# Convolution lanes moved by one 512-token window, with the tap sums begun as their products come

## The chip, the core and the metric

The kernel runs on one core of one Trainium2 chip. The metric is the device time of one execution in microseconds (us), taken as the median of several runs; a profile of one execution, taken by the hardware profiler, lies beside it. The names used below: TensorE (PE in the profile; PEld is its weight load), VectorE (DVE), ScalarE (ACT), GpSimd (POOL) and SyncE (SP), which here only issues DMAs. SBUF is the on-chip memory, PSUM the memory that TensorE writes its results to.

## The reference

The input `x` has 8 sequences of 4096 tokens with 192 channels in float32. First comes a causal convolution over 7 tokens: the 8 heads have 24 channels each, and every head has 7 tap weights, which go through a softmax. Then comes a gated layer on every token:

```
w   = softmax(weight, axis=-1)                      # 8 heads x 7 taps
y_t = sum over k of w[head, k] * x[t - 6 + k]       # zeros ahead of a sequence
out = (relu(y @ w_gate) * (y @ w_val)) @ w_out      # 192 -> 1536 -> 192
```

The output has 32768 rows of 192 values in float32.

## The kernel before, in words

**Tiling.** A window is 512 tokens (`WIN`, line 40). A unit is two windows of one sequence together with the same two windows of the sequence four further on (`UNIT`, line 51), so that 64 channels of either sequence fill the 128 partitions. There are 16 units (`NUNIT`, line 52); four units go through one pair of sequences. The 192 channels are three chunks of 64 (`NCH`).

**A unit on TensorE** has two stages. In the *gate stage* `gate_val` (line 540) goes through two windows; in each, 12 groups of 24 matmuls (line 560) build the gate and the value product of 128 hidden features in two PSUM tiles; ACT takes the relu of one (line 571) and DVE multiplies it with the other into `hT` (line 572). In the *projection stage* `project_turn` (line 575) is called six times, for three output blocks `p` in two turns each, in the order of line 703; each call is 48 matmuls (line 582). After a block's first turn ACT copies two columns (`between_turns`, line 594); after its second, DVE transposes the block out of PSUM (`turn_out`, line 597, its instruction is line 600). `store` (line 605) writes the unit's output through SP. All PSUM tiles come from one pool of four in rotation (line 70).

**The convolution.** TensorE does it for the first two units: `conv_steps` (line 372) for the two windows of unit 0, and `conv` (line 401, its matmuls line 409, its ACT moves line 422, its transposing DMAs line 441) for unit 1, conv(2) for the first 560 tokens ahead of unit 0's projections and conv(3) for the rest between two of them (line 710). From unit 2 on a *lane* does it on the other engines. The lane of unit u+2 runs beside the projections of unit u:

- `lane_load` (line 241) loads x into `x_e` by POOL's DMA queue (line 250); `lane_turn` (line 446) takes 16 tokens of halo from the unit before (line 452), reorders on POOL (line 462) and transposes by eight DMAs on SP (line 464) into `x_r`: channels on partitions, tokens along the row.
- The 3 x 1024 values of a partition are split at `LDVE` = 1280. For the first 1280, ACT writes tap 0 into `acc` (`lane_first`, line 506, instruction line 510) and DVE adds taps 1 to 6 in place (`lane_rest`, line 517), two instructions a tap, of 1024 and 256 elements (line 521): out = x_r * tap + acc, both tensors in SBUF. The sixth tap writes the result into `xc`.
- For the other 1792, ACT writes the product of each tap into its own buffer (`product`, line 486, instruction line 490, two instructions of 768 and 1024 elements), and POOL sums the seven buffers by six additions of 1792 elements (`add`, line 497, instruction line 499), the last of them into `xc`. DVE does the 768-element piece of tap 0 as the last step of its lane (line 531).

**What sets the order.** Nothing reorders: each engine runs its instructions in program order (line 61) and waits by semaphores for data and for free buffers. `TAPS` (line 44) says which products ACT issues after each block's first turn, here taps 6 and 5, then 4 and 3, then 2, 1 and 0; `STEPS` (line 43) says how many of DVE's 13 lane steps stand ahead of each `turn_out`: 6, 5 and 2. POOL's sums for unit u+1 are issued in unit u's part of the main loop (lines 661 to 681), the last one behind the gate stage (line 685); tap 0 being the last product, with DVE's piece the last of its lane, the first sum waits for DVE's line 531. POOL's loads and reorderings stand between these sums in its queue. Each product has one buffer, one `acc` exists, `x_r` has two buffers and `xc` three. In the last two units there is no lane.

Of the kernel before, what the change touches and what calls it, by code (L numbers as in the profile page):

```python
# [15 lines left out]
def kernel(  # L16
# [27 lines left out]
    TAPS = [(6, 5), (4, 3), (2, 1, 0)]  # L44
# [13 lines left out]
    second = [min(t, 2 * UNIT - SUB) for t in range(UNIT, 2 * UNIT, SUB)]  # L58
    GROUPS += [(0, second[:GSUB]), (0, second[GSUB:])]

# [18 lines left out]
    def load_x(g, streams=range(2)):  # L79
# [25 lines left out]
        apool.tile([128, FLAT - LDVE], FP, name=f"prod{jj + 1}")[:, 0 : 2 * D] for jj in range(GSUB)  # L105
# [135 lines left out]
    def lane_load(u, streams=range(2)):  # L241


        bp, t0 = u * UNIT // S, u * UNIT % S
        if u not in xes:
            xes[u] = epool.tile([128, TILES, 2, NCH, 64], F16, name="x_e"), None
        xe, head = xes[u]
        for st in streams:
            row = (bp + NB * st) * S + t0
            nc.gpsimd.dma_start(  # L250
                out=xe[:, :, st, :, :].rearrange("p j c r -> p j (c r)"),
                in_=bass.AP(
                    tensor=x.tensor,
                    offset=x.offset + row * D,
                    ap=[[D, 128], [128 * D, TILES], [1, D]],
                ),
            )
        if 1 in streams and t0 and u - 1 not in xes and u - 1 not in xrs:
            head = const.tile([HALO, 2, NCH, 64], F16, name="head")
            nc.gpsimd.dma_start(  # L260
                out=head[:].rearrange("p s c r -> p s (c r)"),
                in_=bass.AP(
                    tensor=x.tensor,
                    offset=x.offset + (bp * S + t0 - HALO) * D,
                    ap=[[D, HALO], [NB * S * D, 2], [1, D]],
                ),
            )
        xes[u] = xe, head
# [10 lines left out]
    lane_load(2, range(1))  # L279
    for s in (8, 9):  # L280
        pool_halves(s)
    lane_load(2, range(1, 2))
# [82 lines left out]
    xc = {}  # L365
# [30 lines left out]
    def evict(copy, g, ps, c):  # L396
        copy(out=xc[0][:, c, WIN * g : WIN * (g + 1)], in_=ps[:, 0, :])

    def conv(g):
# [40 lines left out]
        for jj, t in enumerate(toks):  # L440
            nc.sync.dma_start_transpose(
                out=xc[1][:, :, t - UNIT : t - UNIT + SUB],
                in_=y[0:SUB, jj].rearrange("p c s r -> p (c s r)"),
            )

    def lane_turn(u):
        xe, head = xes.pop(u)
        xr = rpool.tile([128, NCH, HALO + UNIT], F16, name="x_r")
        if u * UNIT % S == 0:
            nc.gpsimd.memset(xr[:, :, 0:HALO], 0.0)  # L450
        elif head is None:
            nc.gpsimd.tensor_copy(out=xr[:, :, 0:HALO], in_=xrs[u - 1][:, :, UNIT : UNIT + HALO])
        else:
            turned = const.tile([HALO, NCH, 2, 64], F16, name="turned")
            for st in range(2):
                nc.gpsimd.tensor_copy(out=turned[:, :, st, :], in_=head[:, st, :, :])
            nc.sync.dma_start_transpose(
                out=xr[:, :, 0:HALO], in_=turned[:].rearrange("p c s r -> p (c s r)")
            )
        xp = epool.tile([128, TILES, NCH, 2, 64], F16, name="x_p")  # L460
        for st in range(2):
            nc.gpsimd.tensor_copy(out=xp[:, :, :, st, :], in_=xe[:, :, st, :, :])  # L462
        for j in range(TILES):
            nc.sync.dma_start_transpose(
                out=xr[:, :, HALO + 128 * j : HALO + 128 * j + 128],
                in_=xp[:, j].rearrange("p c s r -> p (c s r)"),
            )
        xrs[u] = xr

    def pieces(lo, hi):  # L470


        while lo < hi:
            c, t = lo // UNIT, lo % UNIT
            n = min(UNIT - t, hi - lo)
            yield lo, n, c, t
            lo += n

    def shifted(u, c, k, t, n):
        o = HALO - KW + 1 + k + t  # L480
        return xrs[u][:, c, o : o + n]

    def flat(u):
        return xc[u][:].rearrange("p c t -> p (c t)")

    def product(u, k):
        prods[u, k] = apool.tile([128, FLAT - LDVE], FP, name=f"prod{k}")
        for at, n, c, t in pieces(LDVE, FLAT):
            if k or t == 0:
                nc.scalar.activation(  # L490
                    out=prods[u, k][:, at - LDVE : at - LDVE + n],
                    in_=shifted(u, c, k, t, n),
                    func=ACTF.Copy,
                    scale=tap[:, c, k : k + 1],
                )

    def add(u, k):
        p0 = prods[u, 0]
        nc.gpsimd.tensor_tensor(  # L499
            out=p0[:] if k < KW - 1 else flat(u)[:, LDVE:FLAT],  # L500
            in0=p0[:],
            in1=prods.pop((u, k))[:],
            op=ALU.add,
        )

    def lane_first(u):
        accs[u] = apool.tile([128, LDVE], FP, name="acc")
        xc[u] = xcpool.tile([128, NCH, UNIT], F16, name="xc")
        for at, n, c, t in pieces(0, LDVE):
            nc.scalar.activation(  # L510
                out=accs[u][:, at : at + n],
                in_=shifted(u, c, 0, t, n),
                func=ACTF.Copy,
                scale=tap[:, c, 0:1],
            )

    def lane_rest(u):
        acc = accs.pop(u)
        for k in range(1, KW):
            for at, n, c, t in pieces(0, LDVE):  # L520
                nc.vector.scalar_tensor_tensor(  # L521
                    out=(flat(u) if k == KW - 1 else acc)[:, at : at + n],
                    in0=shifted(u, c, k, t, n),
                    scalar=tap[:, c, k : k + 1],
                    in1=acc[:, at : at + n],
                    op0=ALU.mult,
                    op1=ALU.add,
                )
                yield
        at, n, c, t = next(pieces(LDVE, FLAT))  # L530
        nc.vector.tensor_scalar(  # L531
            out=prods[u, 0][:, 0:n],
            in0=shifted(u, c, 0, t, n),
            scalar1=tap[:, c, 0:1],
            scalar2=None,
            op0=ALU.mult,
        )
        yield

    def gate_val(u, w):  # L540
        h = hpool.tile([128, NFF, 2, WIN], F16, name="hT")
        xcb = xc[u]
        for f in range(NFF):
# [12 lines left out]
            for i, c in order:  # L556
                W = (Wg, Wv)[i]
                for q in range(0, 128, M):
                    for st in range(2):
                        nc.tensor.matmul(  # L560
                            out=pss[i][q : q + M, st, :],
                            lhsT=W[64 * st : 64 * st + 64, c, 128 * f + q : 128 * f + q + M],
                            rhs=xcb[64 * st : 64 * st + 64, c, WIN * w : WIN * (w + 1)],
                            start=(c == 0),
                            stop=(c == NCH - 1),
                            tile_position=(64 * st, q),
                            skip_group_check=True,
                        )
# [76 lines left out]
    xc[0] = xcpool.tile([128, NCH, UNIT], F16, name="xc")  # L645
# [10 lines left out]
    loaded = apool.tile([128, FLAT - LDVE], FP, name="prod0")  # L656
# [4 lines left out]
    for u in range(NUNIT):  # L661
        lane = 1 <= u < NUNIT - 1
        if lane:
            add(u + 1, 1)
        if u == 1:
            lane_load(3)
            add(2, 2)
            add(2, 3)
        if u + 2 < NUNIT:
            lane_turn(u + 2)  # L670
        if u == 0:
            xts[3] = load_x(3)
# [15 lines left out]
        if u == 0:  # L688
            xc[1] = xcpool.tile([128, NCH, UNIT], F16, name="xc")
            conv(2)  # L690
        del xc[u]
# [11 lines left out]
        for p, turn in ((0, 0), (1, 0), (0, 1), (2, 0), (1, 1), (2, 1)):  # L703
# [16 lines left out]
            turn_out(tiles[p], o, p)  # L720
        store(o, bp, w0)
# [30 lines left out]
```

## Time and profile before

| what | value |
|---|---|
| time, median of 3 runs | 763.53 us (763.51 to 763.62) |
| span of the profiled execution | 761.2 us |
| the rest of the time, outside the span | 2.33 us |
| HBM read and written | 29.40 MB, 25.17 MB |
| gate products on DVE, 128x1024 | 383, mean 1221 ns |
| relus on ACT, 128x1024 | 383, mean 1023 ns |
| sums on POOL, 128x1792 | 84, mean 3993 to 4001 ns |
| moves of conv(2) and conv(3) on ACT | 10, 4.6 us together |

The span runs from the first to the last instruction of the profiled execution; the time also has what lies around it. Line numbers (L499) are those of the kernel above. In a timeline row stand the start, the duration, the engine, the line, the operation, and what it writes and reads; rows of neighbours of one kind are merged (x6), and a bracket gives the idle time ahead and what ended it. In a table of stages each engine has its busy time and, in brackets, its instructions; then come the granted clock of TensorE, the share of DMA time and GB/s. A matmul's end is modelled, so a busy TensorE is read by the length of its stages rather than by its busy share.

### The profile page before, as it was taken

Reading aid. Unit: us, or ns where it says so; the run is one execution under the profiler, and the core shown is the slowest. Engines: PE = TensorE matmul, PEld = TensorE weight load, DVE = VectorE, ACT = ScalarE, POOL = GpSimd, SP = SyncE. Lnnn points to the kernel's source line nnn. Section 1 sums busy time; section 2 is a strip of 40 time slices with the busy share of each in tenths; the row PEclk is TensorE's granted clock in tenths of the full one; section 3 lists DMA queues with packets and bytes.
Section 4 is the critical chain, followed back from the end, with each engine's and each line's share of the span. In section 5 each row is a group of like instructions: output and inputs, shape, how many; then the busy total and the mean of one; then the engine's idle time right before and its main releaser. Section 6 shows DMA issues by size and latency. Waiting matters only on the chain.

```text
span 761.2 us, 30408 instructions
## 1 busy us (share of the span) xinstructions
PE 757.1 (99%) x13732; PEld 497.5 (65%) x13732; DVE 669.9 (88%) x634; ACT 604.0 (79%) x671; POOL 425.0 (56%) x200
## 2 busy tenths in 40 slices
PE   9999999999999999999999999999999999999998
PEld 5556666666666666666666666666666666666668
DVE  7879989998998989989899899998999989896691
ACT  7898887878878788787877878788797887874471
POOL 8608749094591936829277391864909558092000
PEclk9999999999999999999999999999999999999999
DMA  9927536054450534516255152442715432030302
GB/s 149 154 56 131 85 82 86 5 121 49 95 76 6 126 42 98 72 27 119 28 106 65 48 102 23 111 59 70 88 14 121 49 88 42 3 84 3 86 3 84
DMA packets 154513, 54.36 MB, mean 71 GB/s; under 512 B 149632, under 2 KB 154384, under 8 KB 154384
## 3 DMA queue, kind: packets, MB, share of 16 engines
q1 hardware_dynamic: 117600, 37.87, 22.6%
q0 software_dynamic: 36352, 14.26, 17.1%
q8 instruction: 107, 1.75, 0.9%
q10 hardware_dynamic: 432, 0.30, 0.1%
q14 instruction: 22, 0.18, 0.1%
HBM read 29.40 MB, written 25.17 MB: 72 GB/s over the span
## 4 chain that ended last, share of the span: by engine, by line
PE 99%; DMA 0%; ACT 0%; issue 0%
PE ps L560 65%; PE ps L582 31%; PE ps L625 2%; PE ps L386 0%; PE ps L409 0%; DMA w<-in_weight_dram 0%; PE ps L195 0%; PE ps L330 0%; PE ps L211 0%; PE ps L205 0%; ACT out_s L636 0%; ACT L129 0%
## 5 line engine op out<-in xcount | busy, mean ns | idle before, releaser
L572 DVE TENSOR_TENSOR hT<-gr,ps 128x1024 f16<-128x1024 f16 (+1 forms) x385 | 468.9, 1218 | 35.3 <-ACT gr L571 8.3
L571 ACT ACTIVATE gr<-ps 128x1024 f16<-128x1024 f32 (+1 forms) x385 | 392.8, 1021 | 116.5 <-PE ps L560 116.5
L499 POOL TENSOR_TENSOR prod<-prod,prod 128x1792 f32<-128x1792 f32 x70 | 279.5, 3993 | 258.6 <-DVE prod L531 230.8
L560 PE MATMUL ps<-xc,Wg 64*64 64x512 f16 (+1 forms) x4464 | 324.3, 376 | 0.0
L560 PE MATMUL ps<-xc,Wv 64*64 64x512 f16 (+1 forms) x4464 | 324.2, 376 | 0.0
L582 PE MATMUL ps<-hT,Wo 64*64 64x512 f16 x4320 | 236.3, 376 | 0.0
L560 PEld LDWEIGHTS <-Wg 64*64 64x64 f16 (+1 forms) x4464 | 163.5, 107 | 85.2
L560 PEld LDWEIGHTS <-Wv 64*64 64x64 f16 (+1 forms) x4464 | 157.0, 106 | 91.4 <-DVE hT L572 0.3
L582 PEld LDWEIGHTS <-Wo 64*64 64x64 f16 x4320 | 153.9, 107 | 78.9 <-issue 0.3
L490 ACT ACTIVATE prod<-x_r,tap 128x1024 f32<-128x1024 f16 (+1 forms) x182 | 175.1, 1044 | 0.0
L521 DVE SCALAR_TENSOR_TENSOR acc<-x_r,tap,acc 128x1024 f32<-128x1024 f16 (+1 forms) x140 | 113.2, 874 | 2.0 <-ACT acc L510 2.0
L600 DVE STREAM_TRANSPOSE out_s<-ps 128x1024 f32<-128x1024 f32 x45 | 56.1, 1247 | 33.3 <-PE ps L582 28.8
L499 POOL TENSOR_TENSOR xc<-prod,prod 128x1792 f16<-128x1792 f32 x14 | 56.0, 4001 | 0.4
L462 POOL COPY x_p<-x_e 128x1536 f16<-128x1536 f16 x28 | 40.3, 1463 | 0.1
L250 POOL DMA_DIRECT2D x_e<-in_x_dram x28 | 25.5, 911 | 0.0
L595 ACT COPY turned_by<-ps 128x2 f32<-128x2 f32 x45 | 7.0, 156 | 21.8 <-PE ps L582 19.9
L521 DVE SCALAR_TENSOR_TENSOR xc<-x_r,tap,acc 128x1024 f16<-128x1024 f16 (+1 forms) x28 | 24.1, 859 | 0.0
L510 ACT ACTIVATE acc<-x_r,tap 128x1024 f32<-128x1024 f16 (+1 forms) x28 | 21.6, 821 | 0.0
L625 PEld LDWEIGHTS <-hT 128*128 128x128 f16 x192 | 15.8, 98 | 0.4 <-issue 0.4
L625 PE MATMUL ps<-Wo,hT 128*128 128x192 f16 x192 | 16.0, 246 | 0.0
L636 ACT COPY out_s<-ps 128x768 f32<-128x768 f32 (+2 forms) x5 | 3.2, 638 | 12.7 <-PE ps L625 12.7
L636 DVE COPY out_s<-ps 128x192 f32<-128x192 f32 x1 | 0.4, 356 | 13.3 <-PE ps L625 13.3
(58 smaller groups left out, 72.4 us busy)
## 6 DMA issues: line engine op xcount, KB each, us to landing
out_dram<-out_s SPq DMA_DIRECT2D x121, 192.0 KB
x_e<-in_x_dram POOLq DMA_DIRECT2D x28, 384.0 KB, 5.3
x_r<-x_p SPq DMA_TRANSPOSE x112
out_dram<-out_s SPq DMA_DIRECT2D x3, 384.0 KB
out_s<-in_x_dram POOLq DMA_DIRECT2D x4, 240.0 KB, 6.7
prod<-in_moe_w_out_dram POOLq DMA_DIRECT2D x1, 576.0 KB, 9.1
prod<-in_x_dram SPq DMA_DIRECT2D x2, 192.0 KB
out_s<-in_x_dram POOLq DMA_DIRECT2D x2, 192.0 KB, 4.9
```

The lines of the kernel that those rows point to most:

```text
L250: nc.gpsimd.dma_start(out=xe[:, :, st, :, :].rearrange("p j c r -> p j (c r)"), in_=bass.AP(tensor=x.tensor, offset=x.offset + row * D, ap ...
L462: nc.gpsimd.tensor_copy(out=xp[:, :, :, st, :], in_=xe[:, :, st, :, :])
L490: nc.scalar.activation(out=prods[u, k][:, at - LDVE : at - LDVE + n], in_=shifted(u, c, k, t, n), func=ACTF.Copy, scale=tap[:, c, k : k + 1],)
L499: nc.gpsimd.tensor_tensor(out=p0[:] if k < KW - 1 else flat(u)[:, LDVE:FLAT], in0=p0[:], in1=prods.pop((u, k))[:], op=ALU.add,)
L510: nc.scalar.activation(out=accs[u][:, at : at + n], in_=shifted(u, c, 0, t, n), func=ACTF.Copy, scale=tap[:, c, 0:1],)
L521: nc.vector.scalar_tensor_tensor(out=(flat(u) if k == KW - 1 else acc)[:, at : at + n], in0=shifted(u, c, k, t, n), scalar=tap[:, c, k : k ...
L560: nc.tensor.matmul(out=pss[i][q : q + M, st, :], lhsT=W[64 * st : 64 * st + 64, c, 128 * f + q : 128 * f + q + M], rhs=xcb[64 * st : 64 * ...
L571: nc.scalar.activation(out=gr[:, sts], in_=pss[0][:, sts], func=ACTF.Relu)
L572: nc.vector.tensor_tensor(out=h[:, f, sts], in0=gr[:, sts], in1=pss[1][:, sts], op=ALU.mult)
L582: nc.tensor.matmul(out=ps[64 * st : 64 * st + 64, b, :], lhsT=Wo[64 * r : 64 * r + 64, f, p, :], rhs=hs[b][64 * r : 64 * r + 64, f, st, :] ...
L600: nc.vector.transpose(out=o[:].rearrange("p t (b d) -> p b t d", b=2)[:, :, :, 32 * p : 32 * p + 32], in_=ps[:].rearrange("p b (t c) -> p ...
L625: nc.tensor.matmul(out=ps[:, i // 2, D * (i % 2) : D * (i % 2) + D], lhsT=h[:, f, st, 128 * q : 128 * (q + 1)], rhs=Wo[:, f, :, :].rearran ...
```

## The change

The lane works on *blocks* of two windows that are shifted by one window against the units: block b has the windows 2b+3 and 2b+4, that is the second window of unit b+1 and the first of unit b+2. There are 15 blocks (0 to 14), and the last has one window, so that the lanes do 29 windows where they did 28. conv(3) goes: TensorE convolves window 2 with conv(2), and window 3 comes from block 0. The lane of block u runs beside the projections of unit u, as the lane of unit u+2 did; its first window is now needed by the second window of the next unit's gate stage, where before the next gate stage had to pass altogether.

The products are issued in tap order: 0 and 1 after the first block's first turn, 2 and 3, then 4 to 6. DVE's piece is that of tap 6. The sums stand in POOL's queue behind all else of the unit, at the end of its turn of the main loop; each waits for its product. The last sum is two instructions of 896 elements, one a window. The next block's reordering and the load of the one after it are issued behind the unit's gate stage, ahead of the sums. Tiles keep their sizes; the window becomes an outer dimension of the accesses (2 x 512, 2 x 128, 2 x 384), and a block that crosses from one sequence to the next has 16 zeros between its windows in `x_r`.

```
-    TAPS = [(6, 5), (4, 3), (2, 1, 0)]
+    TAPS = [(0, 1), (2, 3), (4, 5, 6)]
...
-    FLAT = NCH * UNIT
-    LDVE = 1280
+    LDVE = 640
+    LPOOL = NCH * WIN - LDVE
+    CUT = LDVE - WIN
...
+    NBLOCK = NUNIT - 1
...
+    def windows(b):
+        return [k for k in (2 * b + 3, 2 * b + 4) if k < 2 * NUNIT]
...
+    def second_start(b):
+        return HALO + WIN + HALO * (WIN * (2 * b + 4) % S == 0)
...
+    MINE = [(0, 0, 0, WIN), (WIN, 1, 0, CUT)]
+    POOLS = [(0, 1, CUT, WIN - CUT), (WIN - CUT, 2, 0, WIN)]
...
+    def add(b, k):
+        p0, pk = prods[b, 0], prods.pop((b, k))
+        if k < KW - 1:
+            end = LPOOL * len(windows(b))
+            nc.gpsimd.tensor_tensor(out=p0[:, 0:end], in0=p0[:, 0:end], in1=pk[:, 0:end], op=ALU.add)
+            return
+        for w in range(len(windows(b))):
+            part = slice(LPOOL * w, LPOOL * (w + 1))
+            nc.gpsimd.tensor_tensor(
+                out=xcs[b][:, w, :, :].rearrange("p c t -> p (c t)")[:, LDVE : NCH * WIN],
+                in0=p0[:, part],
+                in1=pk[:, part],
+                op=ALU.add,
+            )
...
+    def window(u, w):
+        if u == 0:
+            return dense[0], w
+        if w == 1:
+            return xcs[u - 1], 0
+        return (xcs[u - 2], 1) if u > 1 else (dense[1], 0)
...
     for u in range(NUNIT):
-        lane = 1 <= u < NUNIT - 1
-        if lane:
-            add(u + 1, 1)
-        if u == 1:
-            lane_load(3)
-            add(2, 2)
-            add(2, 3)
-        if u + 2 < NUNIT:
-            lane_turn(u + 2)
         if u == 0:
-            xts[3] = load_x(3)
+            lane_turn(0)
+            lane_load(1)
...
-        if lane:
-            for k in range(4 if u == 1 else 2, KW - 1):
-                if k == KW - 2 and 1 < u < NUNIT - 3:
-                    lane_load(u + 3, range(1))
-                add(u + 1, k)
-            if 1 < u < NUNIT - 3:
-                lane_load(u + 3, range(1, 2))
         hs = [gate_val(u, w) for w in range(2)]
-        if lane:
-            add(u + 1, KW - 1)
-        if u == 1:
-            lane_load(4)
...
-        if u + 2 < NUNIT:
-            lane_first(u + 2)
-            lane = lane_rest(u + 2)
+        if u < NBLOCK:
+            lane_first(u)
+            lane = lane_rest(u)
+        if u + 1 < NBLOCK:
+            lane_turn(u + 1)
+        if u + 2 < NBLOCK:
+            lane_load(u + 2)
...
                 between_turns(tiles[p])
-                if u == 0 and p == 0:
-                    conv(3)
                 if lane:
                     for k in TAPS[p]:
-                        product(u + 2, k)
-                if u == 0 and p == 1:
-                    psum.tile([128, 2, 512], FP, name="ps")
+                        product(u, k)
...
             turn_out(tiles[p], o, p)
+        if lane:
+            for k in range(1, KW):
+                add(u, k)
         store(o, bp, w0)
```

In the kernel after the change the lines that the prediction names stand elsewhere: sums L517 and, for the last, L521; multiply-adds L543; DVE's product piece L554; products L506; gate products L603; transposes out of PSUM L631.

More of the change, by code (lines that the diff above doesn't have):

```diff
@@ L104 @@
     raw = [
-        apool.tile([128, FLAT - LDVE], FP, name=f"prod{jj + 1}")[:, 0 : 2 * D] for jj in range(GSUB)
+        apool.tile([128, 2 * LPOOL], FP, name=f"prod{jj + 1}")[:, 0 : 2 * D] for jj in range(GSUB)
     ]
@@ L239, with lane_load @@
     xes, xrs, accs, prods = {}, {}, {}, {}
[L241 to L247, printed above, removed]
+    def windows(b):
+        return [k for k in (2 * b + 3, 2 * b + 4) if k < 2 * NUNIT]
+    def lane_load(b, streams=range(2)):
+        n = 4 * len(windows(b))
+        if b not in xes:
+            xes[b] = epool.tile([128, TILES, 2, NCH, 64], F16, name="x_e"), None
+        xe, head = xes[b]
         for st in streams:
-            row = (bp + NB * st) * S + t0
+            row = NB * st * S + WIN * (2 * b + 3)
             nc.gpsimd.dma_start(
-                out=xe[:, :, st, :, :].rearrange("p j c r -> p j (c r)"),
+                out=xe[:, 0:n, st, :, :].rearrange("p j c r -> p j (c r)"),
                 in_=bass.AP(
@@ L278 @@
         pool_halves(s)
-    lane_load(2, range(1))
+    lane_load(0, range(1))
     for s in (8, 9):
         pool_halves(s)
-    lane_load(2, range(1, 2))
+    lane_load(0, range(1, 2))
     mx = const.tile([128, 1], FP)
@@ L396, in evict @@
     def evict(copy, g, ps, c):
-        copy(out=xc[0][:, c, WIN * g : WIN * (g + 1)], in_=ps[:, 0, :])
+        copy(out=dense[0][:, g, c, :], in_=ps[:, 0, :])
     def conv(g):
@@ L459, in lane_turn @@
             )
+        at = second_start(b)
+        if at > HALO + WIN:
+            nc.gpsimd.memset(xr[:, :, at - HALO : at], 0.0)
+        n = 4 * len(windows(b))
         xp = epool.tile([128, TILES, NCH, 2, 64], F16, name="x_p")
         for st in range(2):
-            nc.gpsimd.tensor_copy(out=xp[:, :, :, st, :], in_=xe[:, :, st, :, :])
-        for j in range(TILES):
+            nc.gpsimd.tensor_copy(out=xp[:, 0:n, :, st, :], in_=xe[:, 0:n, st, :, :])
+        for j in range(n):
+            to = HALO + 128 * j if j < 4 else at + 128 * (j - 4)
@@ L464, in lane_turn @@
             nc.sync.dma_start_transpose(
-                out=xr[:, :, HALO + 128 * j : HALO + 128 * j + 128],
+                out=xr[:, :, to : to + 128],
                 in_=xp[:, j].rearrange("p c s r -> p (c s r)"),
             )
[L468 to L503, printed above, removed]
-        )
[L506 to L512, printed above, removed]
+        xrs[b] = xr
@@ new lines, in shifted, with both, result @@
+    def shifted(b, c, k, t, n):
+        o = 1 - KW + k + t
+        row = xrs[b][:, c, HALO + o : HALO + o + n]
+        return bass.AP(
+            tensor=row.tensor,
+            offset=row.offset,
+            ap=[row.ap[0], [second_start(b) - HALO, len(windows(b))], [1, n]],
+        )
+    def both(tile, b, lo, n):
+        return tile[:].rearrange("p (w t) -> p w t", w=2)[:, 0 : len(windows(b)), lo : lo + n]
+    def result(b, lo, n):
+        return xcs[b][:].rearrange("p w c t -> p w (c t)")[:, 0 : len(windows(b)), lo : lo + n]
@@ new lines, with product @@
+    MINE = [(0, 0, 0, WIN), (WIN, 1, 0, CUT)]
+    POOLS = [(0, 1, CUT, WIN - CUT), (WIN - CUT, 2, 0, WIN)]
+    def product(b, k):
+        prods[b, k] = apool.tile([128, 2 * LPOOL], FP, name=f"prod{k}")
+        for at, c, t, n in POOLS[k == KW - 1 :]:
+            nc.scalar.activation(
+                out=both(prods[b, k], b, at, n),
+                in_=shifted(b, c, k, t, n),
+                func=ACTF.Copy,
+                scale=tap[:, c, k : k + 1],
+            )
[12 more added lines that the diff above has]
+                op=ALU.add,
+            )
@@ L513, in lane_first @@
+    def lane_first(b):
+        accs[b] = apool.tile([128, 2 * LDVE], FP, name="acc")
+        xcs[b] = xcpool.tile([128, 2, NCH, WIN], F16, name="xc")
+        for at, c, t, n in MINE:
+            nc.scalar.activation(
+                out=both(accs[b], b, at, n),
+                in_=shifted(b, c, 0, t, n),
                 func=ACTF.Copy,
@@ L529, in lane_rest @@
                 yield
-        at, n, c, t = next(pieces(LDVE, FLAT))
+        k = KW - 1
+        at, c, t, n = POOLS[0]
         nc.vector.tensor_scalar(
-            out=prods[u, 0][:, 0:n],
-            in0=shifted(u, c, 0, t, n),
-            scalar1=tap[:, c, 0:1],
+            out=both(prods[b, k], b, at, n),
+            in0=shifted(b, c, k, t, n),
+            scalar1=tap[:, c, k : k + 1],
             scalar2=None,
```

51 lines of the change are left out of this document (24 added, 27 removed).

## The prediction

> **What bounds the kernel now.** I read the page's engine table first, then the clock row, then the chain that ended last.
>
> ```profile
> span 761.2 us, 30408 instructions
> PE 757.1 (99%) x13732; PEld 497.5 (65%) x13732; DVE 669.9 (88%) x634; ACT 604.0 (79%) x671; POOL 425.0 (56%) x200
> PEclk9999999999999999999999999999999999999999
> PE 99%; DMA 0%; ACT 0%; issue 0%
> ```
>
> TensorE is busy from end to end at the full granted clock, and the chain is TensorE alone. The chain in order of time shows how regular that is; the first four rows are unit 0's projection stage, then the gate stage of unit 1, one later unit and the start of the next, and the gate stage of unit 15.
>
> ```profile
> 40.56 0.99 PE ps L409 x8
> 41.55 2.71 PE ps L582 x48
> 44.27 0.96 PE ps L409 x8
> 45.22 13.07 PE ps L582 x240
> 58.30 31.13 PE ps L560 x576
> ...
> 384.70 31.08 PE ps L560 x576
> 415.78 15.54 PE ps L582 x288
> 431.32 31.08 PE ps L560 x576
> ...
> 711.04 31.08 PE ps L560 x576
> ```
>
> A unit is 31.08 us of gate and value matmuls (two windows of 15.54) and 15.54 us of projection, 46.62 together; the first and the last of the 15 gate stages after unit 0 differ by 0.05. So a gain can only come from matmuls that go, and a loss only from a wait that reaches TensorE. The other engines decide whether one does. Their busy time in the two stages of that unit, then line 499 (POOL's sums) alone, then line 521 (DVE's multiply-adds) alone:
>
> ```profile
> 384.70:415.78 31.08, 31.08 (x580) 20.34 (x576) 28.96 (x25) 24.13 (x24) 28.62 (x11) 1.00 0.61 104
> 415.78:431.32 15.54, 15.54 (x292) 10.42 (x288) 14.02 (x17) 14.47 (x19) 0.00 (x0) 1.00 0.01 3
> ...
> 384.70:415.78 31.08, 23.98 (x6) 1.00 0.61 104
> 415.78:431.32 15.54, 0.00 (x0) 1.00 0.01 3
> ...
> 384.70:415.78 31.08, 0.00 (x0) 1.00 0.61 104
> 415.78:431.32 15.54, 9.72 (x12) 1.00 0.01 3
> ```
>
> The columns are PE, PEld, DVE, ACT, POOL. DVE (14.02 of 15.54) and ACT (14.47) are nearly full in the projection stage, and POOL does nothing there. All six sums lie in the gate stage, all twelve multiply-adds in the projection stage: they never meet.
>
> **What goes: a half convolution on TensorE.** conv(3) is the second L409 row, 0.96 us. The projections around it took 2.71 + 13.07 = 15.78 where other units take 15.54; half of those 0.24 us I give to it. Gain 1.08 us, and its five ACT moves and five transposes go too. That is all there is to win: 0.14%, below the 0.2% (1.5 us) that I take as what a measurement of this kernel can tell from no change.
>
> **What moves: the sums.** Before, tap 0 (with DVE's piece of it) came last, so no sum could start before the lane's end. Now taps 0 and 1 come first. One unit by the timeline, DVE, ACT, POOL:
>
> ```profile
> 417.37 4.86 DVE L521 SCALAR_TENSOR_TENSOR acc<-x_r,tap,acc 128x1024 f32<-128x1024 f16 x6
> 423.67 1.25 DVE L600 STREAM_TRANSPOSE out_s<-ps 128x1024 f32<-128x1024 f32 x1 [1.44 <-PE ps L582]
> 424.84 3.23 DVE L521 SCALAR_TENSOR_TENSOR acc<-x_r,tap,acc 128x1024 f32<-128x1024 f16 x4
> 427.99 1.27 DVE L521 SCALAR_TENSOR_TENSOR xc<-x_r,tap,acc 128x1024 f16<-128x1024 f16 x1
> 429.19 1.24 DVE L600 STREAM_TRANSPOSE out_s<-ps 128x1024 f32<-128x1024 f32 x1
> 430.36 0.44 DVE L521 SCALAR_TENSOR_TENSOR xc<-x_r,tap,acc 128x256 f16<-128x256 f16 x1
> 430.72 0.61 DVE L531 TENSOR_SCALAR prod<-x_r,tap 128x768 f32<-128x768 f16 x1
> 431.44 1.25 DVE L600 STREAM_TRANSPOSE out_s<-ps 128x1024 f32<-128x1024 f32 x1
> 433.07 1.22 DVE L572 TENSOR_TENSOR hT<-gr,ps 128x1024 f16<-128x1024 f16 x1 [0.38 <-ACT gr L571]
> ...
> 418.47 3.84 ACT L490 ACTIVATE prod<-x_r,tap 128x768 f32<-128x768 f16 x4
> ...
> 388.94 2.88 POOL L462 COPY x_p<-x_e 128x1536 f16<-128x1536 f16 x2
> 391.78 12.14 POOL L499 TENSOR_TENSOR prod<-prod,prod 128x1792 f32<-128x1792 f32 x3
> 403.86 0.91 POOL L250 DMA_DIRECT2D x_e<-in_x_dram  x1
> 431.48 3.99 POOL L499 TENSOR_TENSOR prod<-prod,prod 128x1792 f32<-128x1792 f32 x1 [17.81 <-DVE prod L531]
> ```
>
> The first two products (four ACT instructions) end at 418.47 + 3.84 = 422.31, so the first sum starts there and no longer at 431.48. The result of window 2u+3 is needed at the next unit's second window, 431.32 + 15.54 = 446.86. Five sums at 12.14/3 = 4.05 and half a sum (the last is now split by window) end at 422.31 + 20.2 + 2.0 = 444.5. **If nothing slows them**, the sums are 2.3 us early and the new deadline costs nothing.
>
> **What they now lie beside** is the question. From 424.84 on, DVE runs six multiply-adds and a tensor_scalar while POOL sums. The trace has no such overlap, so I bound it by these groups (busy us, mean ns of one), the last two being DVE's gate products in a gate stage with six sums and in one without any:
>
> ```profile
> L499 POOL TENSOR_TENSOR prod<-prod,prod 128x1792 f32<-128x1792 f32 x70 | 279.5, 3993 | 258.6 <-DVE prod L531 230.8 <-ACT prod L490 25.3
> L521 DVE SCALAR_TENSOR_TENSOR acc<-x_r,tap,acc 128x1024 f32<-128x1024 f16 x70 | 88.9, 1271 | 2.0 <-ACT acc L510 2.0
> L521 DVE SCALAR_TENSOR_TENSOR acc<-x_r,tap,acc 128x256 f32<-128x256 f16 x70 | 33.4, 477 | 0.0
> L531 DVE TENSOR_SCALAR prod<-x_r,tap 128x768 f32<-128x768 f16 x14 | 8.6, 612 | 0.0
> L462 POOL COPY x_p<-x_e 128x1536 f16<-128x1536 f16 x28 | 40.3, 1463 | 0.1
> ...
> L572 DVE TENSOR_TENSOR hT<-gr,ps 128x1024 f16<-128x1024 f16 x23 | 28.1, 1221 | 2.0 <-ACT gr L571 0.4
> ...
> L572 DVE TENSOR_TENSOR hT<-gr,ps 128x1024 f16<-128x1024 f16 x23 | 28.1, 1221 | 2.0 <-ACT gr L571 0.4
> ```
>
> Lower end: no cost; the gate products are 1221 ns with sums beside them and without. But they read one operand from SBUF (gr) and one from PSUM; a multiply-add reads both, x_r and acc, from SBUF. Upper end: they exclude each other, a multiply-add waiting for a whole sum of 3993 ns. Rates make me choose an exclusion. A multiply-add goes at (1271 - 477)/768 = 1.03 ns an element over about 0.21 us of fixed time; the tensor_scalar, with one operand, at (612 - 210)/768 = 0.52. So DVE seems to have two ways into SBUF, and a multiply-add fills both. POOL takes 0.95 ns an element with one operand, 2.23 with two, as if it fetched them in turn through one way. If that way is one of DVE's two, both need all of it. The gate products leave it free, which their row allows; it allows separate ways too, so this stays an inference, and the nearest row by kind speaks for no cost.
>
> The Trainium skill, "SBUF — State Buffer", section "Who interferes with whom", states such a rule: a VectorE instruction with two SBUF inputs and a GpSimd instruction that reads SBUF exclude each other for a whole instruction, while one with at most one SBUF input does not contend. On the second half the trace agrees (1221 ns both ways); on the first no run here shows anything. By it the sum would be one of the two exclusive cases below; without it, that of no cost.
>
> **Sum, if a running sum blocks DVE and DVE's adjoining instructions go in a row.** I choose this order because six multiply-adds take 4.86 where their means add to 3 x 1.271 + 3 x 0.477 = 5.24 (the next begins before the last ends), while sums follow each other with 4.05 - 3.99 = 0.05 us between. The first sum runs 422.31 to 426.30; the multiply-add that began at 424.84 waits 1.46. Five then run in a row (4.42) to 430.72; the second sum enters, to 434.71. DVE's transpose goes on beside it; the next multiply-add, ready at 430.36 + 1.46 = 431.82, waits 2.89. The last transpose, which frees the third PSUM tile, and all gate products behind it come 1.46 + 2.89 = 4.35 late. DVE had 0.38 to spare there, so TensorE waits 3.97 a unit. Fourteen full blocks (units 0 to 13): 55.6. Block 14 is half as long and its sums near 2 us; at most some tenths. Span 761.2 - 1.08 + 55.6 = 815.7. The median, 763.53, stands 2.33 over the span: **818**.
>
> **Costed at nothing.** Element counts per lane instruction are unchanged. POOL now has the copies and two loads ahead of the sums in its queue (2.88 + 2 x 0.91 = 4.7 us, and a short halo copy), between the end of the last sums (446.5 to 452) and the next projection at 462: about 5 us of cover, and if it went the first sum would be late by the rest. SP issues the next block's transposes ahead of a unit's stores; both are a stage early. Unit 14 gets a half lane in a projection stage that had none.
>
> **Rivals.**
> - Strict turns: POOL gets the way after every multiply-add. Four more sums then stand ahead of DVE: 1.46 + 4 x 4.0 - 0.38 = 17.1 a unit, 14 x 17.1 = 239, a few more in block 14: about **1,005**. If only the long ones give way, half of that on top, near 890 to 930. For it: a waiting sum is there from the first on. Against: the row above without gaps.
> - Shared pace: both run, at half speed. The 5.55 us of multiply-adds and tensor_scalar double: 5.55 - 0.38 = 5.2 a unit, about **835**.
> - Separate ways: no cost, the sums in time, only conv(3) gone: 760.1 + 2.33 = **762.4**. It decides for "not slower" if the multiply-adds stay at 1271 ns beside sums. For it: the unchanged 1221 ns.
> - Late sums: above 3.99 + 2.3/5.5 = 4.4 us each, TensorE waits at the second window instead; at 5 us it is 3.2 a unit, near 807. In my forecast the sums end about 5.4 late, 0.9 inside a deadline that itself moved by 3.97.
>
> **Chances.** DVE runs in a row, shared pace or late sums (775 to 850): 0.46, of which my forecast 0.30. Turns, strict or partial (850 to 1,015): 0.34. Separate ways: 0.20. The range 775 to 1,015 leaves out the last alone. Faster by over 0.2% needs 762.0 and more than conv(3): 0.03; within: 0.17; slower: 0.80.
>
> **What would show it.** DVE's multiply-adds (now L543) well above 1271 ns, or gaps ahead of them, while sums (L517) run; TensorE's idle at the start of each gate stage, released by DVE's transpose (L631); 14 equal gaps, none in unit 15. I am wrong if multiply-adds keep 1271 ns beside running sums and the units stay 46.62; the order is wrong if sums and multiply-adds alternate.

## The result, and the profile after

The changed kernel takes 1013.5 us (median of 4 runs, 1011.3 to 1015.84) where the kernel before takes 763.58 beside it: a ratio of 1.3271, 95% interval 1.3256 to 1.3287. It is a third slower. The page of the changed kernel, in the lines that answer to those of before:

```profile
span 1009.4 us, 30510 instructions
PE 796.1 (79%) x13724; PEld 499.3 (49%) x13724; DVE 907.6 (90%) x647; ACT 610.7 (60%) x681; POOL 468.4 (46%) x227
PEclk9979969789698896988969979699797997979999
PE 64%; DVE 23%; issue 12%; DVEq 0%; ACT 0%
```

TensorE was 99% busy and the whole chain. Now it is 79% busy, DVE has a quarter of the chain, and the clock row is no longer all nines. One unit shows why. These are its timeline rows for DVE, then POOL, then TensorE at the start of the next gate stage; the projections began at 491.58.

```profile
499.47 1.25 DVE L631 STREAM_TRANSPOSE out_s<-ps 128x1024 f32<-128x1024 f32 x1 [1.44 <-PE ps L613]
500.65 15.79 DVE L543 SCALAR_TENSOR_TENSOR acc<-x_r,tap,acc 128x1024 f32<-128x1024 f16 x4
516.36 4.97 DVE L543 SCALAR_TENSOR_TENSOR xc<-x_r,tap,acc 128x1024 f16<-128x1024 f16 x1
521.25 1.24 DVE L631 STREAM_TRANSPOSE out_s<-ps 128x1024 f32<-128x1024 f32 x1
522.42 0.44 DVE L543 SCALAR_TENSOR_TENSOR xc<-x_r,tap,acc 128x256 f16<-128x256 f16 x1
522.78 0.61 DVE L554 TENSOR_SCALAR prod<-x_r,tap 128x768 f32<-128x768 f16 x1
523.31 1.24 DVE L631 STREAM_TRANSPOSE out_s<-ps 128x1024 f32<-128x1024 f32 x1
...
498.20 22.05 POOL L517 TENSOR_TENSOR prod<-prod,prod 128x1792 f32<-128x1792 f32 x5 [29.69 <-ACT turned_by L626]
523.56 4.11 POOL L521 TENSOR_TENSOR xc<-prod,prod 128x896 f16<-128x896 f32 x2 [3.31 <-DVE prod L554]
...
522.54 1.49 PE L591 MATMUL ps<-xc,Wg 64*64 64x512 f16 x12 [14.13 <-DVE out_s L631]
524.60 1.50 PE L591 MATMUL ps<-xc,Wv 64*64 64x512 f16 x12 [0.56 <-DVE out_s L631]
```

The four multiply-adds that took 3.23 us now take 15.79, for just as long as POOL sums. The groups of single instructions in that stretch say how: the four that met a whole sum, two of 256 elements and two of 1024, each last nearly as long as that sum (3.99 us) and their own time (0.48 and 1.27 us) together.

```profile
L543 DVE SCALAR_TENSOR_TENSOR acc<-x_r,tap,acc 128x256 f32<-128x256 f16 x1 | 4.2, 4229 | 0.0
...
L543 DVE SCALAR_TENSOR_TENSOR acc<-x_r,tap,acc 128x1024 f32<-128x1024 f16 x1 | 5.0, 4980 | 0.0
L543 DVE SCALAR_TENSOR_TENSOR acc<-x_r,tap,acc 128x256 f32<-128x256 f16 x1 | 4.2, 4172 | 0.0
...
L543 DVE SCALAR_TENSOR_TENSOR xc<-x_r,tap,acc 128x1024 f16<-128x1024 f16 x1 | 5.0, 4970 | 0.0
```

The time ahead of them is 0.0: a blocked instruction shows as a long one, not as an idle engine. They go by strict turns, one sum and one multiply-add: in single rows the five sums start at 498.20, 502.29, 507.23, 511.34 and 516.23, and the five multiply-adds end at 503.29, 507.44, 512.34, 516.43 and 521.33, one of each in turn. The transposes beside the same sums keep their 1.24 to 1.25 us. Over the whole span, by the waits view of TensorE:

```profile
PE ps L591 <- DVE out_s L631: 208.5, 30, 14.3
```

The span is 248.2 us longer. 208.5 of it is TensorE's wait for the late transposes: 14.7 a unit in fourteen units, as in the unit above (14.13 + 0.56), and 2.7 at the half block. Another 39.0 is TensorE's own work: 796.1 us busy, against 757.1 with eight matmuls more. These are the stages from that wait on (the number after POOL's is the granted clock):

```profile
507.12:524.60 17.48, 2.79 (x37) 1.34 (x29) 17.48 (x9) 1.54 (x2) 13.94 (x5) 0.64 0.00 0
524.60:556.12 31.52, 31.52 (x544) 19.43 (x547) 27.53 (x23) 22.59 (x23) 7.83 (x7) 0.93 0.73 102
```

After 14 us without work TensorE comes back at a lower clock (0.64 over the first stretch, most of which is the wait, and 0.93 over the rest of the gate stage), and twelve matmuls take 1.49 us instead of 0.85. In narrower stretches of this trace the mean granted clock is 0.77 over the first 6.59 us of the wait (508.41 to 515.00), 0.50 over the rest of it, 0.50 over the first 5.86 us behind it (522.54 to 528.40), and 0.99 from there to 556. The Trainium skill, "TensorE: Matmul & The Clock Gate", Part 1, states that the array falls to half its clock after an idle window of about 3.4 us and needs as long a busy one to return; the 0.50 agrees, and the return took nearer 6 us here, a second wait of 0.56 among them.

### The profile page after: what moved, and what is told of

The parts are those of the page before. It is cut to its first block, busy times and chain, and to the rows that moved or that the text cites. A ratio compares the mean times of both kernels' runs of the same rounds, so it can differ in the third digit from the quotient of the medians.

```text
span 1009.4 us, 30510 instructions
## 1 busy us (share of the span) xinstructions
PE 796.1 (79%) x13724; PEld 499.3 (49%) x13724; DVE 907.6 (90%) x647; ACT 610.7 (60%) x681; POOL 468.4 (46%) x227
## 4 chain that ended last, share of the span: by engine, by line
PE 64%; DVE 23%; issue 12%; DVEq 0%; ACT 0%
PE ps L591 49%; DVE acc L543 17%; PE ps L613 12%; DVE out_s L631 5%; PE ps L656 2%; DVE prod L554 1%; DVE xc L543 1%; PE ps L390 0%; PE ps L196 0%; PE ps L334 0%; PE ps L413 0%; PE ps L212 0%; PE ps L206 0%; ACT out_s L667 0%; DVEq L603 0%
## 5 line engine op out<-in xcount | busy, mean ns | idle before, releaser
L603 DVE TENSOR_TENSOR hT<-gr,ps 128x1024 f16<-128x1024 f16 (+1 forms) x385 | 468.2, 1217 | 57.0 <-PE ps L591 17.7
L517 POOL TENSOR_TENSOR prod<-prod,prod 128x1792 f32<-128x1792 f32 (+1 forms) x75 | 315.7, 4209 | 425.0 <-ACT turned_by L626 387.2
L591 PE MATMUL ps<-xc,Wg 64*64 64x512 f16 (+1 forms) x4464 | 343.6, 395 | 200.5 <-DVE out_s L631 199.8
L591 PE MATMUL ps<-xc,Wv 64*64 64x512 f16 (+1 forms) x4464 | 339.5, 392 | 8.7 <-DVE out_s L631 8.7
L543 DVE SCALAR_TENSOR_TENSOR acc<-x_r,tap,acc 128x1024 f32<-128x1024 f16 (+3 forms) x150 | 304.9, 2096 | 2.0 <-ACT acc L532 2.0
L591 PEld LDWEIGHTS <-Wv 64*64 64x64 f16 (+1 forms) x4464 | 160.4, 110 | 116.9 <-issue 29.7
L506 ACT ACTIVATE prod<-x_r,tap 128x1024 f32<-128x1024 f16 (+2 forms) x195 | 182.8, 1019 | 0.0
L521 POOL TENSOR_TENSOR xc<-prod,prod 128x896 f16<-128x896 f32 x29 | 59.7, 2080 | 49.4 <-DVE prod L554 49.4
L631 DVE STREAM_TRANSPOSE out_s<-ps 128x1024 f32<-128x1024 f32 x45 | 55.8, 1240 | 22.1 <-PE ps L613 18.7
L543 DVE SCALAR_TENSOR_TENSOR xc<-x_r,tap,acc 128x1024 f16<-128x1024 f16 (+3 forms) x30 | 73.1, 2435 | 0.0
L474 POOL COPY x_p<-x_e 128x1536 f16<-128x1536 f16 (+1 forms) x30 | 41.8, 1422 | 0.1
L532 ACT ACTIVATE acc<-x_r,tap 128x1024 f32<-128x1024 f16 (+3 forms) x30 | 22.5, 803 | 0.0
```

What stands on the lines that cost most here:

```text
L474: nc.gpsimd.tensor_copy(out=xp[:, 0:n, :, st, :], in_=xe[:, 0:n, st, :, :])
L506: nc.scalar.activation(out=both(prods[b, k], b, at, n), in_=shifted(b, c, k, t, n), func=ACTF.Copy, scale=tap[:, c, k : k + 1],)
L517: nc.gpsimd.tensor_tensor(out=p0[:, 0:end], in0=p0[:, 0:end], in1=pk[:, 0:end], op=ALU.add)
L521: nc.gpsimd.tensor_tensor(out=xcs[b][:, w, :, :].rearrange("p c t -> p (c t)")[:, LDVE : NCH * WIN], in0=p0[:, part], in1=pk[:, part], op= ...
L543: nc.vector.scalar_tensor_tensor(out=result(b, at, n) if k == KW - 1 else both(acc, b, at, n), in0=shifted(b, c, k, t, n), scalar=tap[:, c ...
L591: nc.tensor.matmul(out=pss[i][q : q + M, st, :], lhsT=W[64 * st : 64 * st + 64, c, 128 * f + q : 128 * f + q + M], rhs=xcb[64 * st : 64 * ...
```

## The experiments

Theory: a sum running on POOL and a multiply-add on DVE exclude each other, by turns. Rival A: the block layout, with its accesses and waits, costs the time. Rival B: the new deadline at the second window does. Smaller rivals stand with their runs. A time given without an interval is that of a single run.

**Without the sums.** Only the last sum stays.

```
-            for k in range(1, KW):
-                add(u, k)
+            add(u, KW - 1)
```

> The changed kernel without POOL's sums of taps 1 to 5 (they are left out; the last sum, in two halves, stays, and it starts after DVE's lane). All else of the change is there: shifted blocks, accesses by window, one half convolution less. Theory (a running sum on POOL and a multiply-add on DVE exclude each other, in strict turns): every multiply-add of 1024 elements is back at 1.27 us, the units at 46.62 us, time 762.4 (761.9 to 762.9). Rival A (the block layout, its accesses or its waits cost the time): it stays near 1,010.

Measured: 764.11 us, ratio to before 1.0003 (0.9994 to 1.0012); the multiply-adds of 1024 elements are back at 1.28 us, and the units at 46.62 from the fourth on. All of the 250 us left with the sums, so rival A falls. The time is 1.2 us above the stated range. In the profile the excess lies at the start: the first gate matmul begins at 8.48 instead of 7.59, a gap of 0.42 stands after unit 0, on which more below, and the next two gate stages are 0.4 longer each.

**The kernel before, with early sums.** Nothing but the tap order.

```
-    TAPS = [(6, 5), (4, 3), (2, 1, 0)]
+    TAPS = [(0, 1), (2, 3), (4, 5, 6)]
...
-            out=prods[u, 0][:, 0:n],
-            in0=shifted(u, c, 0, t, n),
-            scalar1=tap[:, c, 0:1],
+            out=prods[u, KW - 1][:, 0:n],
+            in0=shifted(u, c, KW - 1, t, n),
+            scalar1=tap[:, c, KW - 1 : KW],
```

> The kernel before with nothing but the tap order changed: taps 0 and 1 first, DVE's piece on tap 6, so that POOL's work starts beside DVE's lane as in the changed kernel, with no shifted blocks and no new deadline. Theory of turns: DVE's last transpose of a unit comes 12 to 16 us late behind sums and copies (1.5 for the first sum, then turns with the halo copy, two copies of 1.4 and sums of 4), and TensorE's clock drops in the wait: 940 to 1,010. Rival A (block layout): 763.5. Rival B (the deadline at the second window): 763.5 too, since this kernel does not have it.

Measured: 996.6 us. The old layout with its old deadline is nearly as slow as the new one, so rivals A and B fall as the cause. Its groups show both sides waiting. POOL's halo copy takes 1218 ns (222 before) and its copies of x_e 2021 (1463); DVE's tensor_scalar, which the changed kernel keeps clear of the sums, takes a whole sum too:

```profile
L521 DVE SCALAR_TENSOR_TENSOR xc<-x_r,tap,acc 128x1024 f16<-128x1024 f16 x14 | 67.2, 4797 | 0.0
L531 DVE TENSOR_SCALAR prod<-x_r,tap 128x768 f32<-128x768 f16 x14 | 58.9, 4204 | 0.0
...
L462 POOL COPY x_p<-x_e 128x1536 f16<-128x1536 f16 x28 | 55.9, 2021 | 0.0
L452 POOL COPY x_r<-x_r 128x48 f16<-128x48 f16 x10 | 12.2, 1218 | 0.0
```

**The changed kernel with late sums.** The tap order of before, so that no sum lies beside the lane; the deadline stays.

```
-    TAPS = [(0, 1), (2, 3), (4, 5, 6)]
+    TAPS = [(6, 5), (4, 3), (2, 1, 0)]
...
-        for at, c, t, n in POOLS[k == KW - 1 :]:
+        for at, c, t, n in POOLS[k == 0 :]:
...
-        k = KW - 1
+        k = 0
```

> The changed kernel with the tap order of before (6 and 5 first, DVE's piece on tap 0): no sum can run beside DVE's lane, but the block's first window is still due at the next unit's second window. Theory: multiply-adds at 1.27 us; the sums run from 15.9 us after the projections' start, so the first window's last sum ends near 38.3 and TensorE needs it at 31.3: it waits about 7 us a unit, 14 units, and the clock may drop in it: 860 (850 to 890). If instead something other than the overlap slowed the changed kernel, it stays near 1,010 or goes above.

Measured: 890.2 us, 0.2 above the range. The multiply-adds are back at 1289 ns, and TensorE waits for POOL instead of DVE:

```profile
PE ps L591 <- POOL xc L521: 95.1, 14, 6.9
```

That is 6.8 a unit where 7 was worked out. The 30 us above 860 are the clock: TensorE is busy 788.2 us, 31 more than before. So the deadline is real, and starting the sums early is what it asks for; the early start is what collides.

**Late sums by window.** The same, and POOL sums the first window through all taps before it turns to the second.

```
-            for k in range(1, KW):
-                add(u, k)
+            for w in range(len(windows(u))):
+                for k in range(1, KW):
+                    add(u, k, w)
```

> As the run with late sums, and POOL sums the block's first window through all taps (six additions of 896 elements, about 2.08 us each), then the second. Theory: no sum beside DVE's lane; the first window is done 15.9 + 6 x 2.1 = 28.5 us after the projections' start, 2.8 us ahead of its use, the second at 41.3, POOL's copies and loads end at about 46.2, before the next lane's first multiply-add at 48.4. So nothing waits and one half convolution is gone: 762.4 (762.1 to 762.9), 0.14% under the kernel before. If the copies run into the lane: some us a unit more, 780 or above.

Measured: 763.18 us, ratio 0.9992 (0.9983 to 1.0001). This is 0.3 us above the stated range, but nothing waits: the change's layout works without loss once the sums keep off the lane and come in the order of use. Whether it gains is not told by this interval, so it ran again beside the kernel before.

> The kernel with late sums by window once more, beside the kernel before on one chip, since the first interval (0.9983 to 1.0001) just reached 1. From the first gate matmul to the end its profile had 749.5 us where the profile of before had 750.5, the 1.1 us of the half convolution; the time ahead of that matmul was 7.96 in the one and 7.59 in the other. Theory: that start-up time wanders with the landing of x and has nothing to do with the change: ratio 0.9986, below 1 with its interval. Rival: the changed code starts later by 0.4 us for good: ratio 0.9991 or more.

> The kernel before, unchanged, for a profile on this chip and for the width of the comparison itself: ratio 1.000; first gate matmul anywhere from 7.5 to 8.5 us if the start-up wanders, near 7.6 if it is a property of this kernel; 750.5 us from there to the end.

Measured: 763.62 and 763.63 us, ratios 1.0004 (0.9995 to 1.0013) and 1.0003 (0.9994 to 1.0012). The theory for the first (0.9986) failed, and no gain is left. The chain of late sums by window in this run shows where it went:

```profile
8.69 13.14 PE ps L588 x120
...
42.64 15.69 PE ps L610 x288
58.33 0.74 issue
59.07 2.96 PE ps L588 x49
```

The first gate matmul came at 8.69 (7.96 in the same kernel's profile before, 7.78 in this profile of the kernel before). The start does wander in one and the same kernel: in this profile ACT's cast of x had to wait 0.84 us for its load, in the profile before 0.42. But the rival, a later start for good, is not excluded: the ten profiles of kernels with the new layout begin at 7.8 to 8.7, the three with the old one at 7.6 to 8.0, and the ratio came out on the rival's side. Also, 0.74 us went between unit 0's projections and the next gate stage. SP's queue shows conv(2)'s transposes running right up to it, while POOL's loads of block 2 run too:

```profile
44.25 13.56 SPq L445 DMA_TRANSPOSE xc<-out_s  x5
...
46.37 1.75 POOL L254 DMA_DIRECT2D x_e<-in_x_dram  x2 [0.30 <-POOL x_p L474]
```

**The first load later.**

```
-        if u + 2 < NBLOCK:
+        if 0 < u < NBLOCK - 2:
             lane_load(u + 2)
...
             for w in range(len(windows(u))):
                 for k in range(1, KW):
                     add(u, k, w)
+                if u == 0 and w == 0:
+                    lane_load(2)
```

> The kernel with late sums by window, and in unit 0 POOL issues block 2's loads between the sums of the two windows, in the gate stage that follows, not beside unit 0's projections. In the second profile of that kernel TensorE stood 0.74 us between the projections of unit 0 and the next gate stage, while SP's five transposes of conv(2) took 13.6 us (44.3 to 57.8) beside these loads. If the loads made them late, the five end some us earlier and this wait is gone in the profile: 58.3 to the next gate stage without a gap, median 0.3 to 0.7 us under that of late sums by window, ratio to before 0.9985 to 0.9995. If the transposes are slow by themselves, nothing changes: up to 0.8 us of wait in the profile and ratio 0.9992 to 1.0004.

Measured: 762.61 us, ratio 0.9993 (0.9984 to 1.0002). In its profile the transposes take 7.67 us and the gap is gone:

```profile
43.79 7.67 SPq L445 DMA_TRANSPOSE xc<-out_s  x5
...
42.17 15.66 PE ps L610 x288
57.83 31.08 PE ps L588 x576
```

So the loads had slowed the transposes. Other profiles agree: where the loads start 1.4 to 2.8 us after the first of the five transposes, these take 11.4 to 14.0 us (eight profiles); with copies on POOL (below) the loads start 6.3 us after it, and the five take 8.24; and ten transposes of the kernel before, with no loads beside them, took 15.09, also 1.5 each. From the first gate matmul to the last instruction the profile has 749.4 us, where those of the kernel before have 750.5 and 750.6: the half convolution's gain is there. The medians are 0.9 us apart (762.61 and 763.5), but the interval still reaches 1: that this version beats the kernel before is likely and not shown.

**What it is on POOL that blocks.** First only writes, then one operand read, in place of the sums.

```
-            nc.gpsimd.tensor_tensor(out=p0[:, 0:end], in0=p0[:, 0:end], in1=pk[:, 0:end], op=ALU.add)
+            for _ in range(2):
+                nc.gpsimd.memset(pk[:, 0:end], 0.0)
```

> The changed kernel with each of POOL's sums of taps 1 to 5 replaced by two memsets of the product's buffer (1792 elements each): POOL then only writes SBUF (the sums are left out). The memsets still wait for their products, so they lie beside DVE's lane. Theory, if what is shared is a way to read SBUF: multiply-adds stay at 1.27 us, time 762.4 (762 to 764). Rival (any POOL instruction excludes DVE's lane): multiply-adds of up to 1.3 us plus one memset, several us a unit, 800 or above.

Measured: 771.2 us, above the forecast and below the rival's 800 (the kernel before took 764.75 beside it). DVE's groups, then the memsets:

```profile
L544 DVE SCALAR_TENSOR_TENSOR acc<-x_r,tap,acc 128x1024 f32<-128x1024 f16 x70 | 89.6, 1279 | 2.0 <-ACT acc L533 2.0
L544 DVE SCALAR_TENSOR_TENSOR acc<-x_r,tap,acc 128x256 f32<-128x256 f16 x70 | 33.5, 479 | 0.0
L555 DVE TENSOR_SCALAR prod<-x_r,tap 128x768 f32<-128x768 f16 x14 | 23.7, 1694 | 0.0
...
L518 POOL MEMSET prod<- 128x1792 f32 x140 | 225.4, 1632 | 287.9 <-ACT turned_by L627 283.9
```

The multiply-adds are untouched: POOL's writing does not block them. The tensor_scalar is 1.08 us longer, which the forecast had not. A unit grows by 0.53 us for it (from 46.62 to 47.15), about 7 of the 9 us above the forecast; a gap of 1.17 after unit 0 and a start 0.6 later make up the rest. So writing collides with the tensor_scalar, which goes at half the multiply-add's time an element (0.52 ns against 1.03).

```
-            nc.gpsimd.tensor_tensor(out=p0[:, 0:end], in0=p0[:, 0:end], in1=pk[:, 0:end], op=ALU.add)
+            nc.gpsimd.tensor_copy(out=p0[:, 0:end], in_=pk[:, 0:end])
```

> The changed kernel with each of POOL's sums of taps 1 to 5 replaced by a copy of the product into the first buffer: one operand read in place of two, about 1.7 us in place of 4 (the sums are left out). Theory: a reading instruction excludes the multiply-add, so the turns are shorter: the one waiting for it takes up to 1.7 us more, five or six times, 4 to 6 us a unit: 820 to 860. Rival (only POOL's second operand collides): 762.4.

Measured: 865.2 us. Multiply-adds into acc are 1778 and 1061 ns on average, copies 2024 (busy times that hold the wait). One read operand is enough. TensorE's wait is 62.0 us, 4.4 a unit, as expected; the clock adds 40, which the expectation did not count, and so the time is 5 us above its range.

**The turns.** Each sum in two halves.

```
-            nc.gpsimd.tensor_tensor(out=p0[:, 0:end], in0=p0[:, 0:end], in1=pk[:, 0:end], op=ALU.add)
+            for part in (slice(0, end // 2), slice(end // 2, end)):
+                nc.gpsimd.tensor_tensor(out=p0[:, part], in0=p0[:, part], in1=pk[:, part], op=ALU.add)
```

> The changed kernel with each sum of taps 1 to 5 in two halves of 896 elements, about 2.08 us each; all is computed. Strict turns: each multiply-add waits for one half, so the five that waited for 4 us now wait for 2.1; two more instructions fall into the remaining halves: DVE 10 to 12 us late a unit, 905 to 955. Rival (POOL keeps the way until its queue is empty, or what counts is the total time of the sums): near 1,010 as before. Rival (DVE's adjoining instructions run in a row, the order of my forecast): near 800.

Measured: 948.2 us. POOL's work is the same in total, and the time falls by 65 us: what counts is how long one POOL instruction is and how many DVE instructions meet one. That is what turns say, and neither rival. The groups show the shorter waits:

```profile
L544 DVE SCALAR_TENSOR_TENSOR xc<-x_r,tap,acc 128x1024 f16<-128x1024 f16 x14 | 43.2, 3085 | 0.0
L555 DVE TENSOR_SCALAR prod<-x_r,tap 128x768 f32<-128x768 f16 x14 | 33.9, 2424 | 0.0
```

**One operand on DVE.** The multiply-adds become multiplications.

```
-                nc.vector.scalar_tensor_tensor(
+                nc.vector.tensor_scalar(
...
-                    scalar=tap[:, c, k : k + 1],
-                    in1=both(acc, b, at, n),
-                    op0=ALU.mult,
-                    op1=ALU.add,
+                    scalar1=tap[:, c, k : k + 1],
+                    scalar2=None,
+                    op0=ALU.mult,
```

> The changed kernel with DVE's multiply-adds replaced by multiplications by the tap alone, x_r as the only operand from SBUF (the additions of the previous taps are left out). Alone, such an instruction should take about 0.75 us for 1024 elements and 0.34 for 256. Theory that a multiply-add is caught because it reads two operands, and that DVE uses both ways into SBUF for this instruction too (it moves two elements a cycle): they still wait in turns, 950 to 1,000. Rival (only instructions with two operands in SBUF are caught): no wait, 762.4.

Measured: 971.7 us. Alone such an instruction takes 750 ns for 1024 elements and 350 for 256, as worked out. Beside the sums they wait as the multiply-adds did:

```profile
L543 DVE TENSOR_SCALAR xc<-x_r,tap 128x1024 f16<-128x1024 f16 x14 | 59.4, 4245 | 0.0
```

So it is not the second operand as such. The reading that fits is that DVE uses both its ways into SBUF, for two operands or for one at double pace. The Trainium skill's rule ("SBUF — State Buffer", "Who interferes with whom") names both kinds, with a two-operand instruction caught only by a GpSimd instruction that reads. What the prediction told of that rule lacked a condition: in the Trainium skill an instruction with at most one operand in SBUF stays clear only outside the modes that use both ports. Here runs show each part: 4.97 us beside a sum, 1279 ns beside memsets, 1694 ns for the tensor_scalar beside memsets.

## Why the prediction was wrong

- **What bounds the kernel, and what there was to gain:** right. TensorE's schedule was full. Where the sums are kept off the lane (late sums by window, and with the first load later), conv(3)'s 1.1 us is all that moves; it shows in two profiles and not clear of noise in the times.
- **Sums that nothing slows come in time:** not tested by itself. That a late sum makes TensorE wait at the second window, as one rival had it, was borne out: 6.8 us a unit with late sums.
- **Exclusion, inferred from rates and not from an overlap:** right, as a rule of whole instructions. That a multiply-add fills both of DVE's ways, and that POOL reads through one of them, was read from rates; the memsets, copies and one-operand runs bear it out.
- **"DVE's adjoining instructions go in a row": wrong, and this step failed.** I took it from records that overlap by some hundredths (4.86 us for six) and from 0.05 us between sums. But in those rows neither engine had the other waiting, so they could not tell who comes next when both want to go on. After each multiply-add the waiting sum goes first, and after each sum the waiting multiply-add: the sums and multiply-adds alternate, which is the sign that the prediction had named for a wrong order. Four more sums then stood ahead of DVE in each unit. DVE's last transpose ended 16.1 us late instead of 4.35: at 524.55, 32.97 after the projections' start, where before it was 432.69, 16.91 after.
- **The rival of strict turns had the mechanism,** and its 1,005 is near 1013.5, but by two errors that nearly cancel. It priced 17.1 us of TensorE's wait a unit; 14.7 came. Most of the difference is that part of each multiply-add passes beside a sum: four between five sums took 22.05 - 5 x 3.99 = 2.1 us, not the 3.5 of their means, more than the 0.21 us of fixed time each would explain. And it had no clock: the waits slowed TensorE's later matmuls by about 39 us in all, in none of my sums a term.
- **Costed at nothing:** right for layout, extra half lane and queues in the steady units. Missed at the start: block 2's loads beside conv(2)'s transposes cost 0.74 us in one profile, of a gain of 1.08. Block 14, put at some tenths, cost 2.7.
- **The range** held the time only at its upper edge, and my forecast was a case that did not happen.

## What to carry to other kernels

Work that moves to an idle engine has to be held against what the other engines read and write at that moment, not only against their free time: here POOL was free just when DVE used both its ways into SBUF. Where two engines exclude each other by turns, the bill is the number of short instructions on the critical engine times the length of one long instruction on the other, so keep them in different stages, or make the long ones short. When a wait on TensorE is long enough to lower its clock (4.4 us a unit was, 0.4 was not), price the slow restart too: here 2.2 to 3.3 us for each unit's wait.

## What the runs showed of the hardware that was not expected

The turns are strict even for the shortest instruction: a multiply-add of 256 elements, 0.48 us alone, waited for a whole sum each time (4.2 us), although DVE had its next instruction ready. The clock's price did not grow with the length of the waits. TensorE waited 4.4 us a unit with copies on POOL, 6.8 with late sums, 9.9 with halved sums, 12.5 with one operand, 13.6 in the kernel before with early sums and 14.7 in the changed kernel; its own work was longer than before by 40, 31, 46, 33, 43 and 39 us. With memsets the waits were 0.4 us at most, and the work grew by 2. The mean granted clock does fall with the waits (0.949, 0.939, 0.912, 0.901, 0.892, 0.887), but it counts the waiting time too, so it does not measure the loss. Why the way is not kept for an engine with work at hand stays open. A DVE instruction that reads one operand from SBUF at the slower pace and writes to SBUF was seen beside sums only with its other operand in PSUM (the gate products of the kernel before, 1221 ns), or reading PSUM alone (the transposes); one with SBUF alone was not tried.
